# One input queue for the loads and a choice of VectorE or GpSimd for SBUF-only steps, in an attention and feed-forward kernel

## The chip, the cores and the metric

The kernel runs on one core of one Trainium2 chip. The metric is device time in microseconds (us), lower is better. The engines are named as the profile names them: PE is the TensorE matmul, PEld its weight load, DVE is VectorE, ACT is ScalarE, POOL is GpSimd, SP is SyncE, which only issues DMAs here. PSUM is the memory that PE writes; SBUF is the other on-chip memory.

## The reference, cut to what matters

The input `x` has 2048 tokens of width 512. There are 32 heads of width 16, and four segments of 512 tokens. Each segment has causal attention within itself and, from the second on, reads a memory that the earlier segments left. A gated feed-forward layer (GEGLU, inner width 1792) runs beside it, and a gate per token mixes the two.

```python
phi = lambda t: jnp.where(t > 0, t + 1.0, jnp.exp(t))      # the feature map
g = _sigmoid(beta).reshape(1, H, 1, 1)                     # one number per head
for s in range(N):                                         # N = 4 segments
    p = _softmax(qs @ ks^T * scale + mask)                 # written out as einsums in the reference
    a_dot = p @ vs
    a_mem = (phi(qs) @ M) / (phi(qs) @ z + 1e-06)
    outs.append(g * a_mem + (1.0 - g) * a_dot)
    M = M + phi(ks)^T @ vs;  z = z + sum(phi(ks))
a = concat(outs) @ wo
b = (gelu(x @ w_gate) * (x @ w_up)) @ w_down
gt = _sigmoid((x * gate_w).sum(-1))
return gt * a + (1 - gt) * b
```

## The kernel before

The kernel is a list scheduler. It builds a graph of tasks, each with an engine and an estimated time, simulates the engines and the DMA, and emits each engine's instructions in the order that it found. On the chip every engine then runs its list strictly in that order.

```python
def schedule(self):
    ...
    for e in ENGINES:
        for t in ready[e]:                       # a task may be ready on several engines
            st = max(cur[e], ready_at[t.id])
            ...
            k = (st, -t.prio - ..., t.id)        # the earliest possible start wins
    ...
    t.finish = st + t.est[e]
    avail = t.finish
    if t.nbytes:                                 # a DMA: bytes at one rate, in issue order
        dma_free = max(t.finish + 1.5, dma_free) + t.nbytes / DMA_RATE
        avail = dma_free
```

The first is the loads at the start, with `betaT`, the second layout of `beta`, loaded by four DMAs that write 2 elements (4 bytes) at a time:

```python
for a in range(4):
    rank[0] -= 20.0                              # rank: the wished-for order of the loads
    dma(f"x0_{a}", SP, ..., 131072, bias=rank[0])
wdma("wk", ACT, wk[:], r4(A_wk), 524288)         # ACT issues these two, SP the others
wdma("wq", ACT, wq[:], r4(A_wq), 524288)
...
for g in range(4):                               # no rank: they end up last
    bsrc = A_beta.rearrange("(t g j) -> g t j", g=4, j=2)[g]
    dma(f"betaT{g}", SP, lambda g=g: betaT[32 * g:32 * g + 32, :].rearrange("p (t j) -> p t j", j=2),
        lambda bsrc=bsrc: bsrc.partition_broadcast(32), [], [("betaT", g)], 1024, nonc=True)
```

```python
exp_task(0, "gexp", [
    Instr(lambda e: e.activation(gexp[:], betab[:], ACTF.Exp), ...),
    Instr(lambda e: e.activation(gexpT[:], betaT[:], ACTF.Exp), ...)])
task("gmat", DVE, [...])                         # 1 / (1 + exp), two layouts
```

The DVE work that touches only SBUF: the feature map (two one-input steps and a two-input add per half), the masked copies of K (`kpad`), the masked memory (`mzbd`) and the final add of attention and memory:

```python
task(f"{nm}c{s}_{i}", DVE, [
    Instr(lambda e: e.tensor_scalar(dst[:, t0:t1, :], src[:, t0:t1, :], 0.0, None, ALU.max), ...),
    Instr(lambda e: e.tensor_scalar(ex[:], ex[:], 1.0, None, ALU.min), ...),
    Instr(lambda e: e.tensor_tensor(dst[:, t0:t1, :], dst[:, t0:t1, :], ex[:], ALU.add), ...)])
```

POOL, before, does little but the causal masks (an affine-select on each block of exponentials).

The softmax here doesn't subtract the row's maximum and nothing guards it: scores larger than these inputs give would overflow.

Of the kernel before, what the change touches and what calls it, by code (L numbers as in the profile page):

```python
# [12 lines left out]
ALU = mybir.AluOpType  # L13
# [4 lines left out]
DF = 1792  # L18
# [306 lines left out]

def pool_sel_t(n):
    return 0.17 + n * 0.00105
# [7 lines left out]
def _build(es, nc, A_x, A_wq, A_wk, A_wv, A_wo, A_beta, B_w_gate, B_w_up, B_w_down, gate_w, out):  # L335
# [70 lines left out]

    def mm(g, view, lhsT, rhs, reads, first, last, n, fkey=None):
        return Instr(lambda e: e.matmul(view(), lhsT, rhs, start=first, stop=last),  # L408
                     reads=reads, writes=[fkey if fkey is not None else g.key], est=mm_t(n))
# [60 lines left out]
    for a in range(4):  # L470
        rank[0] -= 20.0
        dma(f"x0_{a}", SP, lambda a=a: xin[:, a, :], lambda a=a: A_x[0, a * 128:(a + 1) * 128, :], [],
            [("hT", 1, a)], 131072, bias=rank[0])
    wdma("wk", ACT, wk[:], r4(A_wk), 524288)
    wdma("wq", ACT, wq[:], r4(A_wq), 524288)
    wdma("gatew", ACT, gatew[:], gate_w.rearrange("(kb p) -> p kb", p=P), 1024, nonc=True)
    wdma("wv", SP, wv[:], r4(A_wv), 524288)
    wdma("beta", SP, betab[:], A_beta.partition_broadcast(P), 8192)
    for g in range(4):
        bsrc = A_beta.rearrange("(t g j) -> g t j", g=4, j=2)[g]  # L480
        dma(f"betaT{g}", SP, lambda g=g: betaT[32 * g:32 * g + 32, :].rearrange("p (t j) -> p t j", j=2),
            lambda bsrc=bsrc: bsrc.partition_broadcast(32), [], [("betaT", g)], 1024, nonc=True)
    wdma(("wg", 0), SP, wg[:, :, 0:half], wgr[:, :, 0:half], 917504)
    xdma(1)
    wdma(("wg", 1), SP, wg[:, :, half:DF], wgr[:, :, half:DF], 917504)
# [7 lines left out]
    for i in range(8):  # L493
# [4 lines left out]
    for kb in range(4):  # L498
# [5 lines left out]
                 [("xT", 0, kb)], 512)  # L504

# [24 lines left out]
    def exp_task(phase, name, instrs, **kw):  # L530
# [3 lines left out]
        t = task(name, ACT, instrs, after=after, **kw)  # L534
        exp_tasks[phase].append(t)
# [23 lines left out]
    def phi_task(nm, s, phase, src, skey, dst, dkey, i):  # L559
# [7 lines left out]
        task(f"{nm}c{s}_{i}", DVE, [  # L567
            Instr(lambda e: e.tensor_scalar(dst[:, t0:t1, :], src[:, t0:t1, :], 0.0, None, ALU.max), tk, dk,
                  dve_t(1024, 4)),
            Instr(lambda e: e.tensor_scalar(ex[:], ex[:], 1.0, None, ALU.min), [("pex", i)], [("pex", i)],  # L570
                  dve_t(1024, 4)),
            Instr(lambda e: e.tensor_tensor(dst[:, t0:t1, :], dst[:, t0:t1, :], ex[:], ALU.add),
                  dk + [("pex", i)], dk, dve_t(1024, 2))])

    def prep(s):
# [11 lines left out]
        if s > 0:  # L587
            for j in range(2):
                task(f"kp{s}_{j}", DVE, [
                    Instr(lambda e, j=j: e.tensor_scalar(kpad[j][sl][:], kT[:], maskc[j][:, 0:1], None, ALU.mult),  # L590
                          [("kT", t) for t in range(4)] + [("c", "mask", j)],
                          [("kpad", j, sl, t) for t in range(4)], dve_t(2048, 4, ap=True))])
# [66 lines left out]
    def memory(s):  # L659
        sl = s % 2  # L660
        if s < NSEG - 1:
# [5 lines left out]
            for i in range(2):  # L667
# [10 lines left out]
                else:  # L678
# [3 lines left out]
                task(f"mzbd{s}_{i}", DVE, [  # L682
                    Instr(lambda e, i=i: e.tensor_tensor(
                        MZbd[:, 2 * i:2 * i + 2, :], MZacc[:, 2 * i:2 * i + 2, :],
                        bdmask[:, :].rearrange("p (o c) -> p o c", o=1).to_broadcast([P, 2, 136]), ALU.mult),
                        [("MZacc", i), ("c", "bd")], [("MZbd", 2 * i), ("MZbd", 2 * i + 1)], dve_t(272))])
# [4 lines left out]
    def attention(s):  # L691
        sl = s % 2
        for t in range(4):
# [53 lines left out]
            def norm():  # L747
# [14 lines left out]
                    Instr(lambda e: e.transpose(dst, obf[i2][:]), [("obf", i2)], dk, dve_t(512))]  # L762
                if s > 0:
# [210 lines left out]
```

## Time and profile before

Three runs have a median of 298.05 us (297.53 to 298.47).

| | before |
|---|---|
| median, us | 298.05 |
| span of the profiled run, us | 296.6 |
| PE busy, us (share) | 277.6 (94%) |
| DVE busy, us | 193.1 (65%) |
| ACT busy, us | 215.6 (73%) |
| POOL busy, us | 102.5 (35%) |

From the page of the kernel before, the line of busy times and the clock that was granted to PE, in tenths of full speed, in 40 slices of 7.4 us:

```profile
PE 277.6 (94%) x2185; PEld 115.2 (39%) x2185; DVE 193.1 (65%) x335; ACT 215.6 (73%) x169; POOL 102.5 (35%) x193
...
PEclk9799999999999999996999999999999999999999
```

PE is the bottleneck, at 94%. What can be won is PE's idle time and the two dips of its clock, in the second slice and near 135 us. The view of waits, for PE of the kernel before (columns: who waited, for whom, us in total, how often, the longest):

```profile
PE psXALL L703 <- ACT pt L711: 4.8, 6, 1.3
PE psW L408 <- DVE hT L834: 2.6, 3, 1.6
PE psW L408 <- DVE otok L650: 2.4, 5, 1.7
PE psW L500 <- DMA hT<-in_A_x_dram: 2.4, 2, 1.9
```

Two stretches of PE's timeline show what the change aims at. Columns: start, duration, engine, line, operation, and in brackets the idle time before it and what ended it. The start:

```profile
7.58 0.23 PE L500 MATMUL psW<-ident,hT 128*128 128x128 bf16 x1 [1.86 <-DMA hT<-in_A_x_dram]
8.30 1.53 PE L500 MATMUL psW<-ident,hT 128*128 128x128 bf16 x13 [0.49 <-DMA hT<-in_A_x_dram]
9.62 1.06 PE L408 MATMUL psW<-xT,wk 128*128 128x512 bf16 x2
10.47 1.06 PE L408 MATMUL psW<-xT,wq 128*128 128x512 bf16 x2
```

`x` is the last thing to arrive, and the first K matmuls take 0.43 us each (two of them pass from 9.62 to 10.47) where warm ones take 0.216. The stage near 130 us:

```profile
133.38 0.39 PE L703 MATMUL psXALL<-qT,kpad_1 32*128 32x512 bf16 x4 [1.35 <-ACT pt L711]
135.42 1.20 PE L408 MATMUL psW<-mzbd,phq 128*128 128x128 bf16 x8 [1.65 <-DVE otok L650]
```

Here PE waits for DVE's `otok`, and directly before it DVE's list holds one of the SBUF-only steps that the change offers to POOL (a final add, at 133.61 us, of 1.15 us).

### The profile page before, as it was taken

To read this page: it belongs to the slowest core of one execution; us is meant where nothing else is said; L and a number is where in the kernel's file an instruction comes from. 1 tells how busy PE (TensorE), PEld (TensorE's weight loads), DVE (VectorE), ACT (ScalarE), POOL (GpSimd) and SP (SyncE) were. 2 spreads that over 40 slices of the span, in tenths; PEclk is the share of its full clock that TensorE was granted. 3 is DMA by queue.
4 is the path that set the end of the run, shared out by engine and by line. 5 is a ranking of instruction groups with operands and counts; after the bars stand their busy time and mean duration, and the time that the engine had idled before them with its cause. 6 is when DMAs were issued, how large, how long until landed. Compare 5 with 4: busy or idle time off the path is not lost.

```text
span 296.6 us, 5371 instructions
## 1 busy us (share of the span) xinstructions
PE 277.6 (94%) x2185; PEld 115.2 (39%) x2185; DVE 193.1 (65%) x335; ACT 215.6 (73%) x169; POOL 102.5 (35%) x193
## 2 busy tenths in 40 slices
PE   5999999998899999987998999997998999997995
PEld 1443433334443344342443334433443334333442
DVE  0388899678988655796427783869616773559431
ACT  2387898889999877877579697687768677667202
POOL 7026773341004346733003334563202334433200
PEclk9799999999999999996999999999999999999999
DMA  7999920000024201002002100110003000000002
GB/s 217 246 338 352 114 49 2 0 1 2 18 55 88 56 24 43 7 2 53 2 5 48 38 0 0 38 39 0 2 1 73 2 0 20 35 20 0 2 0 71
DMA packets 29769, 15.30 MB, mean 52 GB/s; under 512 B 21296, under 2 KB 29744, under 8 KB 29744
## 3 DMA queue, kind: packets, MB, share of 16 engines
q1 hardware_dynamic: 28160, 13.91, 18.8%
q10 hardware_dynamic: 1584, 1.05, 1.2%
q8 instruction: 17, 0.28, 0.4%
q14 instruction: 8, 0.07, 0.1%
HBM read 8.14 MB, written 2.10 MB: 35 GB/s over the span
## 4 chain that ended last, share of the span: by engine, by line
PE 74%; ACT 11%; DVE 9%; DMA 2%; issue 2%; SPq 0%; POOL 0%; ACTq 0%; DVEq 0%
PE psW L408 59%; PE psXALL L703 8%; PE psP L736 6%; ACT pt L711 5%; ACT hT L802 3%; DMA hT<-in_A_x_dram 2%; PE psXALL L408 1%; ACT L711 1%; DVE vaug L425 1%; DVE hT L834 1%; DVE kpad_0 L582 1%; DVE kT L425 1%; DVE tb L744 1%; DVE obf L760 1%; DVE kpad_1 L590 1%
## 5 line engine op out<-in xcount | busy, mean ns | idle before, releaser
L711 ACT ACTIVATE pt<-psXALL 128x2048 bf16<-128x2048 f32 x80 | 150.1, 1876 | 45.0 <-PE psXALL L703 33.5
L723 POOL TENSOR_SCALAR_AFFINE_SELECT pt<-pt 128x512 bf16<-128x512 bf16 (+1 forms) x112 | 83.5, 747 | 171.7 <-ACT pt L711 165.0
L408 PE MATMUL psW<-xT,wu 128*128 128x512 bf16 x224 | 53.0, 380 | 4.0 <-DVE hT L834 2.1
L408 PE MATMUL psW<-xT,wg 128*128 128x512 bf16 x224 | 53.0, 389 | 0.0
L408 PE MATMUL psW<-wd,hT 128*128 128x512 bf16 x210 | 50.7, 380 | 0.0
L834 DVE TENSOR_TENSOR hT<-psW,hT 128x512 bf16<-128x512 f32 x56 | 37.7, 686 | 8.6 <-PE psW L408 8.0
L744 DVE STREAM_TRANSPOSE tb<-psP 128x512 f32<-128x512 f32 x32 | 22.8, 713 | 22.8 <-PE psP L736 22.7
L408 PEld LDWEIGHTS psW<-xT,wg 128*128 128x128 bf16 x224 | 21.0, 100 | 27.2 <-issue 4.9
L408 PEld LDWEIGHTS psW<-xT,wu 128*128 128x128 bf16 x224 | 19.8, 98 | 28.9 <-DVE hT L834 3.2
L408 PEld LDWEIGHTS psW<-wd,hT 128*128 128x128 bf16 x210 | 18.9, 97 | 23.7 <-issue 3.6
L736 PE MATMUL psP<-pt,vaug 128*17 128x256 bf16 (+3 forms) x512 | 23.6, 305 | 0.0
L813 ACT ACTIVATE hT<-psW 128x512 bf16<-128x512 f32 x28 | 16.5, 597 | 8.1 <-PE psW L408 8.1
L862 DVE TENSOR_SCALAR ost<-psW,omgt 128x512 bf16<-128x512 f32 x12 | 8.7, 743 | 16.7 <-PE psW L408 16.7
L703 PE MATMUL psXALL<-qT,kpad_1 32*128 32x512 bf16 (+3 forms) x256 | 16.1, 305 | 2.6 <-ACT pt L711 2.4
L703 PE MATMUL psXALL<-qT,kpad_0 32*128 32x512 bf16 (+3 forms) x256 | 15.8, 301 | 2.4 <-ACT pt L711 2.4
L408 PE MATMUL psW<-xT,wk 128*128 128x512 bf16 x64 | 17.0, 395 | 0.1
L408 PE MATMUL psW<-xT,wq 128*128 128x512 bf16 x64 | 16.6, 388 | 0.3 <-DVE qT L425 0.3
L650 DVE TENSOR_TENSOR otok<-psW,ndsc 128x512 bf16<-128x512 f32 x12 | 7.6, 683 | 13.2 <-PE psW L408 13.1
L408 PE MATMUL psW<-wo,oT 128*128 128x512 bf16 x60 | 15.8, 380 | 0.0
L408 PE MATMUL psW<-wv,xT 128*128 128x512 bf16 x64 | 15.5, 380 | 0.0
L736 PEld LDWEIGHTS psP<-pt,vaug 128*17 128x17 bf16 x512 | 10.1, 90 | 13.4 <-issue 6.6
L425 DVE CAST hT<-psW 128x512 bf16<-128x512 f32 x20 | 13.2, 676 | 2.6 <-PE psW L408 2.6
(90 smaller groups left out, 252.6 us busy)
## 6 DMA issues: line engine op xcount, KB each, us to landing
out_dram<-ost SPq DMA_DIRECT2D x16, 128.0 KB, 1.7
wg<-in_B_w_gate_dram SPq DMA_DIRECT2D x2, 896.0 KB, 7.7
wu<-in_B_w_up_dram SPq DMA_DIRECT2D x2, 896.0 KB, 8.2
wd<-in_B_w_down_dram SPq DMA_DIRECT2D x1, 1792.0 KB, 14.9
wk<-in_A_wk_dram ACTq DMA_DIRECT2D x1, 512.0 KB, 4.2
hT<-in_A_x_dram SPq DMA_DIRECT2D x4, 128.0 KB, 5.0
wq<-in_A_wq_dram ACTq DMA_DIRECT2D x1, 512.0 KB, 6.1
wv<-in_A_wv_dram SPq DMA_DIRECT2D x1, 512.0 KB, 8.5
```

Of the source, the lines that this page charges most:

```text
L408: return Instr(lambda e: e.matmul(view(), lhsT, rhs, start=first, stop=last), reads=reads, writes=[fkey if fkey is not None else g.key], e ...
L425: alts[DVE] = [Instr(lambda e: e.tensor_copy(dst(), src()), reads=reads, writes=writes, est=dve_t(n))]
L650: Instr(lambda e, gn=gn, qt=qt: e.tensor_tensor(otok[:, qt, :].rearrange("p (h e) -> p h e", e=16), gn.f32()[:, :].rearrange("p (h e) -> p ...
L703: instrs.append(Instr(lambda e, t=t, g=g, j=j, kb=kb, ncol=ncol, c0=c0: e.matmul(X[g][:, c0:c0 + ncol], kpad[j][sl][32 * g:32 * g + 32, t, ...
L711: prev_exp[0] = exp_task(s, f"exp{s}_{t}{name}", [Instr(lambda e: e.activation(PT[slot][:], XALL[:, :].rearrange("p (g c) -> p g c", g=4), ...
L723: minstrs.append(Instr(lambda e, view=view, pat=pat: e.affine_select(out=view, in_=view, compare_op=ALU.is_ge, fill=0.0, base=0, pattern=p ...
L736: instrs.append(Instr(lambda e, q=q, kb=kb, slot=slot, c0=c0, h=h: e.matmul(Pb[32 * q:32 * q + 17, 128 * kb:512], Vaug[sl][:, kb, h, :], P ...
L744: task(f"pvt{s}_{t}_{j}", DVE, [Instr(lambda e: e.transpose(Tb[i2][:, j, :], Pb[:, :]), [("P",)], [("Tb", i2, j)], dve_t(512))])
L802: t = task(f"gelu{s}_{f0}", ACT, [Instr(lambda e, hv=hv: e.activation(hv, hv, ACTF.Gelu_apprx_tanh), hk, hk, act_t(512 * n, False) + (0.0 ...
L813: lambda e, g=g, ft=ft, s=s: e.activation(hT[s % 2][:, ft, :], g.f32()[:, :], ACTF.Gelu_apprx_tanh),
L834: task(f"Um{s}_{ft}", DVE, [Instr(lambda e, g=g, ft=ft: e.tensor_tensor(hT[sl][:, ft, :], g.f32()[:, :], hT[sl][:, ft, :], ALU.mult), [g.k ...
L862: DVE: [Instr(lambda e, view=view, gt=gt, tile=tile: e.tensor_scalar(ostage[tile][:], view(), omgt[:, gt:gt + 1], None, ALU.mult), rd, [(" ...
```

## The change

It has two intents. The first is to have `x` land sooner: all input loads go on SP's queue in one order, `x` first in two larger loads, and the small loads of the gates follow the weights of Q, K and V. A few more idle matmuls keep PE's clock up until `x` is there. The second is to unload DVE: each SBUF-only step becomes its own task with two alternatives, and the scheduler takes whichever engine can start it first. The diff, cut to its core:

```diff
+def pool_t(n, two=False):
+    return 0.2 + n * (0.0022 if two else 0.0011)

+    def either(name, fn, reads, writes, dve, pool, **kw):
+        return S.add(Task(name, {DVE: [Instr(fn, reads, writes, dve)], POOL: [Instr(fn, reads, writes, pool)]}, **kw))

-    for a in range(4):
+    for a in range(2):
...                                       # x in two loads of 256 KB
-    wdma("wk", ACT, wk[:], r4(A_wk), 524288)
-    wdma("wq", ACT, wq[:], r4(A_wq), 524288)
-    wdma("gatew", ACT, gatew[:], ...)
+    wdma("wk", SP, wk[:], r4(A_wk), 524288)
+    wdma("wq", SP, wq[:], r4(A_wq), 524288)
     wdma("wv", SP, wv[:], r4(A_wv), 524288)
+    wdma("gatew", SP, gatew[:], ...)
     wdma("beta", SP, betab[:], A_beta.partition_broadcast(P), 8192)
     for g in range(4):
+        rank[0] -= 20.0
         dma(f"betaT{g}", SP, ...,
-            ..., [], [("betaT", g)], 1024, nonc=True)
+            ..., [], [("betaT", g)], 1024, nonc=True, bias=rank[0])
     wdma(("wg", 0), SP, wg[:, :, 0:half], wgr[:, :, 0:half], 917504)
+    wdma(("wg", 1), SP, wg[:, :, half:DF], wgr[:, :, half:DF], 917504)
     xdma(1)
-    wdma(("wg", 1), SP, wg[:, :, half:DF], wgr[:, :, half:DF], 917504)

-        task(f"{nm}c{s}_{i}", DVE, [ max, min, add ])             # abridged
+        either(f"{nm}r{s}_{i}", max,  ..., dve_t(1024, 4), pool_t(1024))
+        either(f"{nm}m{s}_{i}", min,  ..., dve_t(1024, 4), pool_t(1024))
+        either(f"{nm}a{s}_{i}", add,  ..., dve_t(1024, 2), pool_t(1024, True))
...                                       # likewise kpad (in halves), mzbd, the final add (nadd)
```

(The diff also adds three warm matmuls before the first K matmul and 1.3 us to the estimate of one exp in each segment after the first.) With these estimates the scheduler moves 28 steps to POOL: 13 one-input steps of 128x1024, and 15 with two inputs (6 feature-map adds, 7 final adds of 128x512, 2 memory masks). And because every estimate enters one simulation, the whole order changes.

More of the change, by code (lines that the diff above doesn't have):

```diff
@@ L469, in _build @@
     xin = hT[1][:, 0:4, :]
-    for a in range(4):
+    for a in range(2):
         rank[0] -= 20.0
-        dma(f"x0_{a}", SP, lambda a=a: xin[:, a, :], lambda a=a: A_x[0, a * 128:(a + 1) * 128, :], [],
-            [("hT", 1, a)], 131072, bias=rank[0])
-    wdma("wk", ACT, wk[:], r4(A_wk), 524288)
-    wdma("wq", ACT, wq[:], r4(A_wq), 524288)
-    wdma("gatew", ACT, gatew[:], gate_w.rearrange("(kb p) -> p kb", p=P), 1024, nonc=True)
+        dma(f"x0_{a}", SP, lambda a=a: xin[:, 2 * a:2 * a + 2, :],
+            lambda a=a: A_x[0, a * 256:(a + 1) * 256, :].rearrange("(t p) d -> p t d", p=P), [],
+            [("hT", 1, 2 * a), ("hT", 1, 2 * a + 1)], 262144, bias=rank[0], issue=0.45)
+    wdma("wk", SP, wk[:], r4(A_wk), 524288)
+    wdma("wq", SP, wq[:], r4(A_wq), 524288)
     wdma("wv", SP, wv[:], r4(A_wv), 524288)
+    wdma("gatew", SP, gatew[:], gate_w.rearrange("(kb p) -> p kb", p=P), 1024, nonc=True)
     wdma("beta", SP, betab[:], A_beta.partition_broadcast(P), 8192)
@@ L480, in _build @@
         bsrc = A_beta.rearrange("(t g j) -> g t j", g=4, j=2)[g]
+        rank[0] -= 20.0
         dma(f"betaT{g}", SP, lambda g=g: betaT[32 * g:32 * g + 32, :].rearrange("p (t j) -> p t j", j=2),
-            lambda bsrc=bsrc: bsrc.partition_broadcast(32), [], [("betaT", g)], 1024, nonc=True)
+            lambda bsrc=bsrc: bsrc.partition_broadcast(32), [], [("betaT", g)], 1024, nonc=True, bias=rank[0])
     wdma(("wg", 0), SP, wg[:, :, 0:half], wgr[:, :, 0:half], 917504)
+    wdma(("wg", 1), SP, wg[:, :, half:DF], wgr[:, :, half:DF], 917504)
     xdma(1)
-    wdma(("wg", 1), SP, wg[:, :, half:DF], wgr[:, :, half:DF], 917504)
     wdma(("wu", 0), SP, wu[:, :, 0:half], wur[:, :, 0:half], 917504)
@@ L492, in _build @@
                              [("P",)], 0.43)], bias=5001.0)
-    for i in range(8):
+    for i in range(9):
         gw = Grp(banks)
@@ L504, in _build @@
                  [("xT", 0, kb)], 512)
+    task("warmE", PE, [Instr(lambda e: e.matmul(Pb[:, :], warm[:, 0:128], warm, start=True, stop=True), [wkey],
+                             [("P",)], 0.3) for _ in range(3)], bias=4.0,
+         after=[t for t in S.tasks if t.name == "x0t3"])
     c = [Instr(lambda e: e.memset(maskc[0][:], 0.0), writes=[("c", "mask", 0)], est=0.1)]
@@ L534, in exp_task @@
         t = task(name, ACT, instrs, after=after, **kw)
+        if phase > 0 and name.endswith("_0A0"):
+            t.est[ACT] += 1.3
         exp_tasks[phase].append(t)
@@ L566, in phi_task @@
                                                tk, [("pex", i)], act_t(1024, False))])
-        task(f"{nm}c{s}_{i}", DVE, [
-            Instr(lambda e: e.tensor_scalar(dst[:, t0:t1, :], src[:, t0:t1, :], 0.0, None, ALU.max), tk, dk,
-                  dve_t(1024, 4)),
-            Instr(lambda e: e.tensor_scalar(ex[:], ex[:], 1.0, None, ALU.min), [("pex", i)], [("pex", i)],
-                  dve_t(1024, 4)),
-            Instr(lambda e: e.tensor_tensor(dst[:, t0:t1, :], dst[:, t0:t1, :], ex[:], ALU.add),
-                  dk + [("pex", i)], dk, dve_t(1024, 2))])
+        either(f"{nm}r{s}_{i}", lambda e: e.tensor_scalar(dst[:, t0:t1, :], src[:, t0:t1, :], 0.0, None, ALU.max),
+               tk, dk, dve_t(1024, 4), pool_t(1024))
+        either(f"{nm}m{s}_{i}", lambda e: e.tensor_scalar(ex[:], ex[:], 1.0, None, ALU.min), [("pex", i)],
+               [("pex", i)], dve_t(1024, 4), pool_t(1024))
+        either(f"{nm}a{s}_{i}", lambda e: e.tensor_tensor(dst[:, t0:t1, :], dst[:, t0:t1, :], ex[:], ALU.add),
+               dk + [("pex", i)], dk, dve_t(1024, 2), pool_t(1024, True))
     def prep(s):
@@ L588, in prep @@
             for j in range(2):
-                task(f"kp{s}_{j}", DVE, [
-                    Instr(lambda e, j=j: e.tensor_scalar(kpad[j][sl][:], kT[:], maskc[j][:, 0:1], None, ALU.mult),
-                          [("kT", t) for t in range(4)] + [("c", "mask", j)],
-                          [("kpad", j, sl, t) for t in range(4)], dve_t(2048, 4, ap=True))])
+                for i in range(2):
+                    tt = (2 * i, 2 * i + 1)
+                    either(f"kp{s}_{j}{i}", lambda e, j=j, i=i: e.tensor_scalar(
+                        kpad[j][sl][:, 2 * i:2 * i + 2, :], kT[:, 2 * i:2 * i + 2, :], maskc[j][:, 0:1], None,
+                        ALU.mult), [("kT", t) for t in tt] + [("c", "mask", j)],
+                        [("kpad", j, sl, t) for t in tt], dve_t(1024, 4, ap=True), pool_t(1024))
         for tile in range(4):
@@ L681, in memory @@
                 task(f"mzacc{s}_{i}", DVE, [first], grp=gm)
-                task(f"mzbd{s}_{i}", DVE, [
-                    Instr(lambda e, i=i: e.tensor_tensor(
-                        MZbd[:, 2 * i:2 * i + 2, :], MZacc[:, 2 * i:2 * i + 2, :],
-                        bdmask[:, :].rearrange("p (o c) -> p o c", o=1).to_broadcast([P, 2, 136]), ALU.mult),
-                        [("MZacc", i), ("c", "bd")], [("MZbd", 2 * i), ("MZbd", 2 * i + 1)], dve_t(272))])
+                either(f"mzbd{s}_{i}", lambda e, i=i: e.tensor_tensor(
+                    MZbd[:, 2 * i:2 * i + 2, :], MZacc[:, 2 * i:2 * i + 2, :],
+                    bdmask[:, :].rearrange("p (o c) -> p o c", o=1).to_broadcast([P, 2, 136]), ALU.mult),
+                    [("MZacc", i), ("c", "bd")], [("MZbd", 2 * i), ("MZbd", 2 * i + 1)], dve_t(272),
+                    pool_t(272, True))
     pt_next = [0]
@@ L762, in norm @@
                     Instr(lambda e: e.transpose(dst, obf[i2][:]), [("obf", i2)], dk, dve_t(512))]
+                task(f"norm{s}_{t}", DVE, ins)
                 if s > 0:
-                    ins.append(Instr(lambda e, t=t: e.tensor_tensor(oT[sl][:, t, :], oT[sl][:, t, :], ott[i2][:],
-                                                                    ALU.add), ok + dk, ok, 0.7))
-                task(f"norm{s}_{t}", DVE, ins)
+                    either(f"nadd{s}_{t}", lambda e, t=t: e.tensor_tensor(oT[sl][:, t, :], oT[sl][:, t, :],
+                                                                         ott[i2][:], ALU.add),
+                           ok + dk, ok, 0.5, pool_t(512, True))
             a0 = fill("A0", [(0, 0, 512, 0)], [0])
```

## The prediction

> What bounds the kernel now. The page gives PE 277.6 us busy of 296.6 (94%); the chain that ended last is 74% PE, 11% ACT, 9% DVE. So only PE's idle 19 us and its cold-clock time can be won. PE's timeline places the idle time:
> - Start: 1.3 us, then about 2.6 us for x (four loads, the last lands at 8.25 us, sharing DMA with wk and wq). Afterwards PE runs cold: matmuls at 0.43 us against 0.216, until 12.1 us.
> - 74 to 81 us: 2.0 us (V eviction behind a gelu on ACT, then DVE's numerators).
> - 130 to 136 us: 3.0 us (exp, then DVE's otok, queued behind a 1.15 us final add); the clock falls to 0.75 and 12 matmuls take 4.4 us instead of 2.7.
> - After gelus: 1.05 (157 us), 0.79 (226 us); 1.6 at 204; 1.6 at 273 (DVE); end about 3 us.
>
> What the change does.
> 1. x goes first, alone, in two loads on one queue, then wk, wq, wv. 512 KB at the 340 GB/s seen later is 1.5 us; x should land near 5 us instead of 8.25. More warm matmuls bridge it. The first K matmul should start at 7 to 7.5 us instead of 9.6, warm. Gain 2 to 3.5 us. Cost: x of segment 1 now queues behind both gate halves and the tiny gate and beta loads; I estimate it at 17 to 21 us, needed at about 20: risk of a stall up to 1.5 us.
> 2. By the instruction orders, about 30 steps move from DVE to POOL: 13 one-input 1024-wide steps, 6 two-input adds, 7 final adds, 2 memory masks. DVE loses about 19 of 193 us (0.42 to 0.7 each). POOL's affine-select of 512 takes 0.65, of 1024 1.1 us, so one-input steps should take about 1.3; for two inputs the Trainium skill, "GPSIMD Engine Reference", section 3.1, states 2.6 cycles an element: an estimate of 2.4 us per 1024. POOL grows from 102 to about 145 us. The skill's "SBUF — State Buffer", "two separate sides", says that GpSimd and a DVE operation with two SBUF inputs or in a two-port mode exclude each other; the trace agrees in kind (an add of mean 0.62 took 1.15 beside a mask). So some DVE steps lengthen and some masks come 1 to 2 us late, mostly absorbed by six buffers.
> 3. The schedule reorders: memory and numerators of segment 1 leave the gelu phase, whose up-projections then run unbroken (gain about 1.7); they land in the stage near 110 us, where ACT's exps are denser than PE's work, so I expect about 2 us idle there instead of the 3 us and the cold clock (gain 1 to 2). Five up-projections, instead of three, cover the table load and first exp after the second gelu (gain 1). DVE waits near 165 and 273 shrink (gain 1 to 1.5).
>
> Sum: gains 7.5 to 10, new losses 1 to 3. Predicted 291.0 us, 8 in 10 between 287.0 and 295.0. Faster by over 2% (under 292.1): 0.60; within 2%: 0.37; slower: 0.03.
>
> What would show it: x landed near 5 us; K matmuls at 0.216 us from the start; PE busy little changed but idle near 12 us; DVE near 175, POOL near 145; no clock dip at 130 to 140; the wait for ACT after the second gelu gone.
>
> What would make it wrong: x of segment 1 late; POOL adds much over 2.4 us or masks delayed so that attention waits for POOL; the numerator stage near 110 us idling PE long enough to drop the clock again; the scheduler's order fitting the chip badly.

## More of the kernel before

`beta` is 32 numbers, and the kernel needs it in two layouts; two small ACT exps and five tiny DVE steps use `beta` and `betaT`.

## The result, and the profile after

The changed kernel is slower: a median of 314.8 us (314.29 to 316.64, 4 runs) against 298.26 (297.53 to 298.51, 4 runs) for the kernel before, with the outputs correct in both. The ratio is 1.057, with a 95% interval of 1.0523 to 1.0617. Ratios are the mean time of one kernel's runs over that of the other's runs of the same rounds, so they are not quite the ratio of the medians that are quoted. Executions over 1.5% slower than the fastest of the same kernel are left out of the means.

| | before | after | predicted |
|---|---|---|---|
| median, us | 298.26 | 314.8 | 291.0 |
| span of the profiled run, us | 296.6 | 312.6 | |
| PE busy, us | 277.6 | 282.5 | little changed |
| span less PE busy, us | 19.0 | 30.1 | about 12 |
| DVE busy, us | 193.1 | 188.7 | about 175 |
| POOL busy, us | 102.5 | 162.7 | about 145 |
| mean granted clock | 0.983 | 0.966 | |

From the page of the changed kernel, the same lines as before:

```profile
PE 282.5 (90%) x2189; PEld 114.9 (37%) x2189; DVE 188.7 (60%) x316; ACT 214.5 (69%) x166; POOL 162.7 (52%) x221
...
PEclk9959999999999999887999999999779999999999
```

PE lost both ways: 11.1 us more idle, and 4.9 us more busy, as its clock dips in three places, near 20, 135 and 225 us (a slice is 7.8 us here). Those are the places of the stories below. PE's waits, after:

```profile
PE psXALL L719 <- DVE gtmp L561: 6.3, 1, 6.3
PE psW L416 <- DVE hT L851: 6.1, 7, 3.3
PE psXALL L719 <- ACT pt L727: 4.5, 8, 1.8
PE psW L416 <- DVE kT L433: 3.5, 2, 3.2
PE psP L752 <- POOL pt L739: 1.5, 2, 0.7
```

Three waits of over 3 us are new: 6.3 (at 18 us), 3.2 (at 141 us) and 3.3 (at 224 us).

**The start.** `x` now lands near 5 us and K's matmuls run warm from 7.46 us, as predicted. Then ACT stops. ACT's timeline after:

```profile
8.54 0.60 ACT L430 ACTIVATE kT<-psW 128x512 bf16<-128x512 f32 x1 [1.84 <-PE psW L416]
10.98 0.23 ACT L554 ACTIVATE gexp<-betab 128x32 f32<-128x32 bf16 x1 [1.84 <-DMA betab<-in_A_beta_dram]
17.25 0.21 ACT L555 ACTIVATE gexpT<-betaT 128x8 f32<-128x8 bf16 x1 [6.05 <-DMA betaT<-in_A_beta_dram]
17.37 0.58 ACT L430 ACTIVATE qT<-psW 128x512 bf16<-128x512 f32 x1
...
18.81 1.88 ACT L727 ACTIVATE pt<-psXALL 128x2048 bf16<-128x2048 f32 x1 [0.38 <-PE psXALL L719]
```

The two gate exps stand in ACT's list between the first K eviction and the evictions of Q and K that attention needs. They wait for `betaT` until 17.25 us, so the copy of Q out of PSUM waits too. PE's wait is put down to DVE's `gtmp`, a gate step that ended at 17.95 us, but the matmul that it ends in reads `qT`, and the eviction of `qT` by ACT ended at the same moment (17.37 + 0.58 = 17.95): the releaser in such a line is inferred, and what the instruction reads decides. DVE's list stops too, for 7.7 us, as its five gate steps wait for `gexpT`. The first attention exp starts at 18.81 us instead of 15.22 before. The chain of waits shows the load behind it, from its issue to its landing (columns: start, duration, what):

```profile
7.56 9.58 DMA betaT<-in_A_beta_dram
...
17.25 0.22 ACT gexpT L555
...
18.09 0.62 PE psXALL L719 x4
```

Four loads of 512 bytes each take until 17.1 us. Busy times by windows of 2 us (columns: busy us of each engine, then the granted clock, the share of the 16 DMA engines that was busy, and GB/s):

```profile
10.00:12.00 2.00, 1.75 (x9) 0.59 (x6) 0.00 (x0) 0.23 (x1) 0.00 (x0) 1.00 0.06 1
12.00:14.00 2.00, 0.00 (x0) 0.00 (x0) 0.00 (x0) 0.00 (x0) 0.00 (x0) 1.00 0.03 0
14.00:16.00 2.00, 0.00 (x0) 0.00 (x0) 0.00 (x0) 0.00 (x0) 0.00 (x0) 0.78 0.54 190
16.00:18.00 2.00, 0.00 (x0) 0.00 (x0) 0.44 (x4) 0.75 (x3) 0.00 (x0) 0.50 0.98 376
```

For 4 us the input queue moves next to nothing, with a DMA share of 0.03 to 0.06, about one engine of the 16; then no engine computes at all; and the clock falls to 0.50 after the idle time. The packets that the trace records, by size and microsecond of the span (a count, not a view of the profile):

```
us   packets started
 9   68 of 1024 B, 171 of 2 B, 44 of 64 B, 80 of 4 B
10   107 of 4 B, 22 of 64 B, 11 of 2 B
11   110 of 4 B
12   57 of 4 B
13   90 of 4 B
14   94 of 4 B, 56 of 1792 B
15   28 of 4 B, 156 of 1792 B
```

`betaT` is 4 loads x 32 partitions x 4 runs of 4 bytes, 512 such packets (some of the 566 of 4 B counted here are not `betaT`'s: up to 18 in a microsecond start before any `betaT` load is issued). They take 7 to 8 ns each, and their times add up to 0.4 to 0.8 us in each microsecond, less than one of the 16 engines can give; in the trace about a third of them (107 of 316 between 10 and 14 us) overlap the next. Small size alone doesn't explain the rate: the 512 packets of 2 B, which are `gatew`, went faster, 330 of them in the microsecond from 8 us. The gate weights (1792 B), which stand behind `betaT` on the same queue, start at 14.2 us, when most of its packets are through.

**POOL.** The groups of moved instructions after, by shape (columns: busy us and mean ns of one, then POOL's idle time before them and what ended it):

```profile
L582 POOL TENSOR_SCALAR phq<-qT 128x1024 bf16<-128x1024 bf16 x4 | 11.5, 2872 | 0.6 <-PE psW L416 0.6
L584 POOL TENSOR_SCALAR pex<-pex 128x1024 bf16<-128x1024 bf16 x4 | 11.2, 2809 | 0.6 <-ACT pex L580 0.6
L586 POOL TENSOR_TENSOR phq<-phq,pex 128x1024 bf16<-128x1024 bf16 x5 | 10.9, 2182 | 0.0
L605 POOL TENSOR_SCALAR kpad_1<-kT,maskc 128x1024 bf16<-128x1024 bf16 x3 | 8.8, 2940 | 3.8 <-ACT kT L430 3.0 <-DVE kT L433 0.9
```

A one-input step takes 2.8 to 2.9 us on POOL. The scheduler was told 0.2 + 1024 x 0.0011 = 1.33, and the prediction said 1.3. A two-input step takes 2.18, where the scheduler was told 2.45 and the prediction 2.4. What the 2.8 does is seen before the wait at 141 us:

```profile
131.75 2.77 POOL L582 TENSOR_SCALAR phq<-qT 128x1024 bf16<-128x1024 bf16 x1
134.48 0.63 POOL L739 TENSOR_SCALAR_AFFINE_SELECT pt<-pt 128x512 bf16<-128x512 bf16 x1
135.09 2.76 POOL L582 TENSOR_SCALAR phq<-qT 128x1024 bf16<-128x1024 bf16 x1
137.82 2.11 POOL L586 TENSOR_TENSOR phq<-phq,pex 128x1024 bf16<-128x1024 bf16 x1
137.88 2.60 DVE L586 TENSOR_TENSOR phq<-phq,pex 128x1024 bf16<-128x1024 bf16 x1 [3.89 <-POOL phq L582]
140.40 0.68 DVE L433 CAST kT<-psW 128x512 bf16<-128x512 f32 x1
141.14 0.82 PE L416 MATMUL psW<-xT,wu 128*128 128x512 bf16 x2 [3.24 <-DVE kT L433]
```

Read from the top: POOL does two slow `max` steps. DVE's next step is the add that needs the second, so DVE, the engine that was to be relieved, stands idle for 3.89 us. It then starts that add beside POOL's own add of the other half, and takes 2.60 us for what takes 0.68 alone. Only then can it evict K, and PE waits 3.24 us for the bank. The wait at 224 us, likewise:

```profile
213.41 2.91 DVE L605 TENSOR_SCALAR kpad_1<-kT,maskc 128x1024 bf16<-128x1024 bf16 x2
213.76 2.28 POOL L586 TENSOR_TENSOR phq<-phq,pex 128x1024 bf16<-128x1024 bf16 x1
...
219.39 2.12 POOL L586 TENSOR_TENSOR phq<-phq,pex 128x1024 bf16<-128x1024 bf16 x1
219.72 1.84 DVE L774 TENSOR_TENSOR sc_0<-recip,gdT 128x32 f32<-128x32 f32 x1
...
224.48 1.89 PE L416 MATMUL psW<-xT,wu 128*128 128x512 bf16 x4 [3.27 <-DVE hT L851]
```

A DVE step of 128x32, which took 0.19 us at 129.48 us, takes 1.84 us and ends with POOL's add. The evictions behind it come late, and PE waits. This is why DVE's busy time fell by only 4.4 us although 28 steps left it: the steps that stayed got longer. (In e2, below, where the 28 steps are back on DVE in the same order, they take about 16 us by their means, and DVE's total is 189.2. So the steps that stayed took about 16 us more here.)

### The profile page after: what moved, and what is told of

The parts are those of the page before. It is cut to its first block, busy times and chain, and to the rows that moved or that the text cites. A ratio compares the mean times of both kernels' runs of the same rounds, so it can differ in the third digit from the quotient of the medians.

```text
span 312.6 us, 5382 instructions
## 1 busy us (share of the span) xinstructions
PE 282.5 (90%) x2189; PEld 114.9 (37%) x2189; DVE 188.7 (60%) x316; ACT 214.5 (69%) x166; POOL 162.7 (52%) x221
## 4 chain that ended last, share of the span: by engine, by line
PE 67%; POOL 11%; DVE 8%; ACT 4%; DMA 4%; issue 3%; SPq 2%; ACTq 0%; DVEq 0%; POOLq 0%
PE psW L416 54%; PE psXALL L719 7%; PE psP L752 5%; POOL pt L739 4%; POOL exsT L634 3%; DMA betaT<-in_A_beta_dram 3%; ACT pt L727 3%; POOL phq L582 3%; SPq L447 1%; PE psXALL L416 1%; DVE hT L851 1%; DVE obf L776 1%; POOL kpad_0 L605 1%; DVE tb L760 1%; DMA oT<-otok 1%
## 5 line engine op out<-in xcount | busy, mean ns | idle before, releaser
L739 POOL TENSOR_SCALAR_AFFINE_SELECT pt<-pt 128x512 bf16<-128x512 bf16 (+1 forms) x112 | 85.2, 763 | 107.7 <-ACT pt L727 99.9
L416 PE MATMUL psW<-xT,wu 128*128 128x512 bf16 x224 | 55.3, 391 | 9.4 <-DVE hT L851 5.9
L719 PE MATMUL psXALL<-qT,kpad_0 32*128 32x512 bf16 (+3 forms) x256 | 16.3, 308 | 7.4 <-DVE gtmp L561 6.3
L719 PE MATMUL psXALL<-qT,kpad_1 32*128 32x512 bf16 (+3 forms) x256 | 16.3, 309 | 3.5 <-ACT pt L727 3.5
L416 PE MATMUL psW<-wv,xT 128*128 128x512 bf16 x64 | 17.3, 410 | 0.7 <-DVE ost L879 0.5
L433 DVE CAST hT<-psW 128x512 bf16<-128x512 f32 x22 | 14.6, 677 | 3.7 <-PE psW L416 3.5
L416 PE MATMUL psW<-xT,wq 128*128 128x512 bf16 x64 | 15.8, 380 | 0.8 <-DMA wq<-in_A_wq_dram 0.5
L781 POOL TENSOR_TENSOR oT<-oT,ott 128x512 bf16<-128x512 bf16 x7 | 8.2, 1174 | 16.0 <-DVE ott L778 15.0
## 6 DMA issues: line engine op xcount, KB each, us to landing
wg<-in_B_w_gate_dram SPq DMA_DIRECT2D x2, 896.0 KB, 12.5
```

The costliest lines, as they stand in the source:

```text
L416: return Instr(lambda e: e.matmul(view(), lhsT, rhs, start=first, stop=last), reads=reads, writes=[fkey if fkey is not None else g.key], e ...
L433: alts[DVE] = [Instr(lambda e: e.tensor_copy(dst(), src()), reads=reads, writes=writes, est=dve_t(n))]
L719: instrs.append(Instr(lambda e, t=t, g=g, j=j, kb=kb, ncol=ncol, c0=c0: e.matmul(X[g][:, c0:c0 + ncol], kpad[j][sl][32 * g:32 * g + 32, t, ...
L739: minstrs.append(Instr(lambda e, view=view, pat=pat: e.affine_select(out=view, in_=view, compare_op=ALU.is_ge, fill=0.0, base=0, pattern=p ...
L781: either(f"nadd{s}_{t}", lambda e, t=t: e.tensor_tensor(oT[sl][:, t, :], oT[sl][:, t, :], ott[i2][:], ALU.add), ok + dk, ok, 0.5, pool_t(5 ...
```

## The experiments

The theory had two independent parts. S: the start loses because the gate exps stand in ACT's list before the evictions and wait for `betaT`. P: the rest loses because steps on POOL are slow and block DVE. The rivals were R, the new order is bad in itself, whatever the engines do; D, the loads alone are at fault (what queues behind the tiny packets); and, within P, whether the one-input steps (longer than thought) or the two-input steps (which exclude DVE) do the harm. Two kinds of edit were used. In the first the changed kernel's schedule is computed as it is, and one thing is then moved in the finished order or between the two engines; the rest of the order stays, and the emitter adds the waits that the new order needs. In the second an estimate or the code is changed and the schedule computed anew, which changes the order too.

All kernels gave correct outputs. The runs were made on four chips, each beside the kernel before, whose median was 297.76 to 298.61 us; a difference of under 1 us between two is not read.

### e1_gexp_later: the gate steps later in the order

```diff
-    for t in S.schedule():
+    order = S.schedule()
+    late = [t for t in order if t.name in ("gexp", "gmat")]
+    order = [t for t in order if t not in late]
+    at = [t.name for t in order].index("gexs0")
+    order[at:at] = late
+    for t in order:
```

The loads stay where the change put them; only the two ACT exps and the five DVE steps are emitted later.

> The schedule of the changed kernel is kept; only the two gate exponentials on ScalarE and the five small gate steps on VectorE, which wait for the late beta load, are moved behind the fourth exp of the first attention stage. Every DMA stays where it is. Theory A (in-order engines ScalarE and VectorE stood 6 us behind the beta load, 17.25 us): the first exp starts at 12 to 13 us instead of 18.8, and the time falls by 4 to 6 us, to about 310. Rival (the loads themselves are late, not the wait on them): the PE waits for DMA instead and the time falls by under 2 us.

Measured: 309.53 us (309.24 to 310.11), ratio 1.0404 (1.0381 to 1.0426). The wait of 6.3 us is gone from PE's waits. So 5.3 of the 16.5 us come from the place of these seven small instructions in the order. A new wait appears, though: 2.8 us for `xT`, the input of segment 1, which stands behind the tiny packets and the gate weights on the queue, and the clock falls to 0.83 over 20 to 30 us. That is rival D, and e6 takes it up.

### e2_all_dve: no step on POOL

```diff
+    for t in order:
+        if len(t.alts) == 2 and DVE in t.alts and POOL in t.alts:
+            t.eng = DVE
```

> The order is kept, but the 29 steps that the scheduler gave to GpSimd run on VectorE at the same place in the order; the beta loads stay. Theory B (GpSimd one-input steps of 2.8 us and the port exclusion delay masks, kT, phq and the up-projection evictions): PE idle of about 10 us at 42 to 49, 131, 141 and 224 us goes, time falls by 8 to 11 us to about 305. Rival (the order of the scheduler is bad whatever the engine; VectorE gets 19 us more work): falls by under 4 us.

Measured: 302.34 us (301.69 to 302.93), ratio 1.0159 (1.0133 to 1.0185). Moving the 28 steps (the expectation miscounted them as 29) back to DVE, in the same order, is worth 12.5 us, a little more than the 8 to 11 expected, and the clock dips near 140 and 220 us are gone. DVE's busy time is 189.2 us, against 188.7 with POOL's help: the 28 steps cost DVE nothing net.

### e3_both: both edits

> Both edits, order otherwise kept. If A and B are all of the loss and add up: 314.8 minus 5 minus 10, about 299 to 301, near the kernel before. If there is a third cause (order, x of segment 1 late): stays above 303.

The edit is that of e1 and of e2 together. Measured: 298.7 us (297.66 to 299.69), ratio 1.0047 (1.0006 to 1.0087). The two parts make 16.1 us together and 17.7 one by one, so they are nearly additive, and between them they account for nearly the whole loss. Rival R is refuted as the cause of the slowdown: this is the changed kernel's own order, but for the seven small steps, and it is within 1% of the kernel before. That the order is a good one is not shown by this; b1 below finds one that is about 7 us faster.

### a1_beta_late: the tiny loads at the end of the queue, scheduled anew

```diff
     for g in range(4):
-        rank[0] -= 20.0
         dma(f"betaT{g}", SP, ...,
-            ..., [], [("betaT", g)], 1024, nonc=True, bias=rank[0])
+            ..., [], [("betaT", g)], 1024, nonc=True)
```

> The four tiny beta loads go to the end of the input queue as before (one line undone), and the scheduler makes its order anew; GpSimd steps stay. Theory A with the tiny loads also holding up the queue: the gate weights land near 15 us instead of 20, the first exp starts near 12 us, time 308 to 310. Rival: same as in the moved-exponential run would mean that the queue hold-up itself costs nothing.

Measured: 306.67 us (304.68 to 308.99), ratio 1.0308 (1.025 to 1.0366). The start was repaired, but this is a partial miss: the same wait came back in another place. The line of PE's timeline in a1_beta_late:

```profile
36.84 1.46 PE L416 MATMUL psW<-xT,wg 128*128 128x512 bf16 x3 [4.96 <-ACT exs L622]
```

Its chain of waits goes from there to `gexpT` on ACT and to a `betaT` load that took 8.76 us after its issue at 27.65. The scheduler still believes that 1024 bytes need next to nothing, so it again put the gate exps before the loads had landed. The fault is the estimate, not only the place in the queue.

### e4_one_dve and e5_two_dve: which kind of step

The order stays. In e4 the 13 one-input steps go back to DVE and the 15 two-input steps stay on POOL; e5 is the reverse.

```diff
+    ONE = ("pqr", "pqm", "pkr", "pkm", "kp")
+    TWO = ("pqa", "pka", "mzbd", "nadd")
+    for t in order:
+        if len(t.alts) == 2 and DVE in t.alts and POOL in t.alts:
+            if t.name.startswith(ONE):        # e5: TWO
+                t.eng = DVE
```

> Order of the changed kernel kept, beta loads kept; the 13 one-input steps (2.8 us each on GpSimd) go back to VectorE, the 15 two-input ones (2.1, 1.2 and 0.7 us) stay on GpSimd. If the cost is the long one-input steps holding up GpSimd's own queue (masks, phq, kT): most of the 12.5 us comes back, about 304 to 306. If it is the exclusion of VectorE's two-input steps while GpSimd does a two-input step: little comes back, 311 to 314.

> The reverse: the 15 two-input steps go back to VectorE, the 13 one-input steps stay on GpSimd. If GpSimd's own queue is the cost: 309 to 313, PE idle near 131 and 141 us stays. If exclusion by two-input steps is the cost: 303 to 306, and the PE idle of 3.3 us near 224 us goes.

Measured: e4 305.91 us (305.68 to 306.4), ratio 1.0277 (1.0256 to 1.0297); e5 309.76 us (309.12 to 310.19), ratio 1.04 (1.0379 to 1.0421). Against 314.8 the one-input steps are worth 8.9 us and the two-input steps 5.0, which add up to 13.9 where both together gave 12.5. Each of the two stalls follows one kind. In e4 PE's waits for `kT` fall from 3.5 us to 0.2, and the wait before the matmul of the second stall stays:

```profile
217.02 1.04 PE L416 MATMUL psW<-xT,wu 128*128 128x512 bf16 x4 [3.27 <-DVE hT L851]
```

In e5 it is the first that stays, and the second becomes shorter (2.0 us is the longest of its kind):

```profile
139.23 0.61 PE L416 MATMUL psW<-xT,wu 128*128 128x512 bf16 x2 [2.74 <-DVE kT L433]
```

So both kinds harm, the one-input steps more, and in different places.

### e6_beta_mid: the tiny loads behind the input of segment 1

The order and engines are those of e3 (no POOL steps). In addition the four `betaT` loads move behind `x` of segment 1, just before the up weights, and what needs them moves back accordingly.

```diff
+    move(("betaT0", "betaT1", "betaT2", "betaT3"), "w_('wu', 0)")
+    move(("gexp", "gmat", "GdT0"), "gexs1")
```

> The run with both edits (298.7) had 2.5 us of PE waiting for x of segment 1 at 20 us and a cold clock after it, and the input queue moved nothing but 4-byte packets from 10 to 14.5 us. Here the four beta loads also go behind x of segment 1, ahead of the up weights, and what needs them behind that; all steps on VectorE. If the tiny loads hold up the whole queue: gate weights land some 4.5 us sooner, the PE wait at 20 us goes, no cold clock at 20 to 30 us, time 294 to 296. If x of segment 1 is late because it queues behind both gate halves: wait stays, time 298 to 299.

Measured: 295.78 us (295.54 to 296.33), ratio 0.9935 (0.9918 to 0.9952), 2.9 us under e3. The stretch at which e3 waited for the input, first in e3_both, then in e6_beta_mid:

```profile
22.88 3.75 PE L416 MATMUL psW<-xT,wq 128*128 128x512 bf16 x8 [2.49 <-DMA xT<-in_A_x_dram]
```

```profile
23.32 1.90 PE L416 MATMUL psW<-xT,wq 128*128 128x512 bf16 x8
```

Eight matmuls take 3.75 us in e3, after an idle time and at a granted clock of 0.57 (mean from 23 to 27 us), and 1.90 in e6, where the clock in that stretch is 1.00. The hold-up by the tiny packets is still there (the DMA share over 20 to 25 us is 0.20), but nothing that PE needs stands behind it. So D is a real but smaller part: about 3 us.

### m1_micro: single steps, alone and side by side

The kernel before, followed by a tail that runs single steps of 128x1024 (bf16) on POOL and DVE, alone, then together. Its time (334.58 us) says nothing; only the tail's lines are read. In the pairs DVE starts 0.2 to 0.4 us after POOL. Each entry is a single sample, and the profiler's spans on POOL are rough.

```diff
+        PH = [(p_ts, None), (p_tt, None), (p_ts5, None), (p_tt5, None), (p_tsm, None), (p_cp, None), (p_sel, None),
+              (None, d_ts), (None, d_tt), (None, d_ps),
+              (p_ts, d_ts), (p_ts, d_tt), (p_ts, d_ps), (p_tt, d_ts), (p_tt, d_tt), (p_tt, d_ps),
+              (p_sel, d_ts), (p_sel, d_tt), (p_sel, d_ps)]
```

> Not for its time: the kernel before, with single steps of GpSimd and VectorE after its end, each alone and then together (VectorE starting about 0.3 us later). Expected alone on 128x1024 bf16: GpSimd one input 2.8, two inputs 2.1, select 1.1; VectorE one input 0.4, two inputs 0.7, from PSUM 0.7. Together: VectorE's two-input step grows to the end of GpSimd's two-input step (about 2.3 us) and of the select; VectorE's step from PSUM is not touched. Open: whether VectorE's one-input step, and its two-input step beside a GpSimd one-input step, are touched[...].

Some lines of the tail's timeline in m1_micro: a one-input POOL step, a two-input one and a select alone; then DVE's two-input step alone and beside POOL's two-input step:

```profile
295.76 2.77 POOL L913 TENSOR_SCALAR pt<-pt 128x1024 bf16<-128x1024 bf16 x1 [17.14 <-DMA out_dram<-ost]
298.68 2.11 POOL L914 TENSOR_TENSOR pt<-pt 128x1024 bf16<-128x1024 bf16 x1
...
308.07 1.05 POOL L919 TENSOR_SCALAR_AFFINE_SELECT pt<-pt 128x1024 bf16<-128x1024 bf16 x1
...
310.35 0.68 DVE L922 TENSOR_TENSOR hT<-hT 128x1024 bf16<-128x1024 bf16 x1
...
323.48 2.11 POOL L914 TENSOR_TENSOR pt<-pt 128x1024 bf16<-128x1024 bf16 x1 [0.36 <-DVE hT L921]
...
323.84 2.30 DVE L922 TENSOR_TENSOR hT<-hT 128x1024 bf16<-128x1024 bf16 x1
```

All of them, in us:

| POOL step | alone | DVE one-input beside it | DVE two-input (SBUF) beside it | DVE with one PSUM input beside it |
|---|---|---|---|---|
| none | | 0.42 | 0.68 | 0.68 |
| one-input max | 2.77 | 0.96 | 1.36 | 0.68 |
| two-input add | 2.11 | 2.17 | 2.30 | 0.68 |
| select | 1.05 | 1.08 | 1.22 | 0.68 |

At 512 elements the one-input step took 1.49 us and the two-input step 1.15, so the slopes are (2.77 - 1.49) / 512 = 2.5 ns and (2.11 - 1.15) / 512 = 1.9 ns per element of a partition. The multiplication by the mask column took 2.85, and a plain copy 1.04. So on POOL a step with one tensor and a scalar costs more than one with two tensors, and of those measured only copy and select are cheap. Beside a two-input add or a select, a DVE step on SBUF ends only after POOL's does. Beside the one-input step it takes 0.5 to 0.7 us more than alone and ends well before POOL does. A DVE step with a PSUM operand is not touched at all. That answers the question left open: DVE's one-input step on SBUF is touched too.

This splits the harm as the stalls do: the one-input steps hurt mainly by their length (the scheduler's 1.33 against 2.8, so what needs them is ready 1.5 us later than planned), the two-input steps by holding DVE up.

### b1_all_dve, b2_true, b4_cheap: mended estimates, scheduled anew

In all three the `betaT` loads stand behind `x` of segment 1 and have a truer cost in the scheduler's DMA model, 700000 bytes each, an estimate that makes the four 8.5 us long at the model's rate.

```diff
     wdma("beta", SP, betab[:], A_beta.partition_broadcast(P), 8192)
+    wdma(("wg", 0), ...); wdma(("wg", 1), ...); xdma(1)      # moved up from below
     for g in range(4):
         rank[0] -= 20.0
-        dma(f"betaT{g}", SP, ..., 1024, nonc=True, bias=rank[0])
+        dma(f"betaT{g}", SP, ..., 700000, nonc=True, bias=rank[0])
```

b1 has only the DVE alternative. b2 keeps both, with the measured POOL costs, `0.2 + n * (0.0019 if two else 0.0025)`. b4 has those costs too but lets only the final adds and memory masks choose (six final adds went to POOL).

> Candidate version: all of the change's start (x first, one queue, warm matmuls, estimate of the table load), the beta loads behind x of segment 1 with a truer cost in the scheduler's estimate, no GpSimd alternative, and the scheduler orders anew. Expected 292 to 295, below both kernels and a little below the frozen order (295.8), because the order is made for the engines that run it. If the order of the scheduler does not matter: 295 to 296.

> As the candidate, but the GpSimd alternatives stay and their estimate is set to what was measured (0.2 + 2.5 ns an element for one input, 1.9 for two). If the cause was only the wrong estimate: as good as the candidate or better, 290 to 294. If holding up masks and VectorE's exclusion cost by themselves: worse than the candidate, 296 to 302.

> As the candidate, but the final add (1.17 us) and the memory mask (0.7 us) may go to GpSimd, with the measured estimate. Six final adds go there. VectorE loses about 4 us of work and some of it waits for the exclusion: within 1 us of the candidate.

Measured:

| | median, us (range) | ratio (95%) | POOL busy, us | DVE busy, us |
|---|---|---|---|---|
| b1_all_dve | 288.98 (288.54 to 290.58) | 0.9703 (0.9669 to 0.9736) | 102.6 | 191.0 |
| b2_true | 300.19 (299.0 to 301.52) | 1.007 (1.0028 to 1.0113) | 146.6 | 196.3 |
| b4_cheap | 290.57 (290.06 to 290.82) | 0.9744 (0.9724 to 0.9765) | 110.3 | 187.4 |

b1 beats both kernels: 9.4 us under the kernel before, and 3 us below the range that was expected. It is also 6.8 us under e6 (295.78; other chip, but the ratios' intervals, 0.9669 to 0.9736 and 0.9918 to 0.9952, lie far apart), which has the same loads and no POOL step but the order that was made for the wrong estimates. So that order, too, costs something against one made for the engines that run it. From b1's page, the busy times and the clock, which no longer dips anywhere:

```profile
PE 270.0 (93%) x2151; PEld 114.6 (40%) x2189; DVE 191.0 (66%) x342; ACT 215.3 (75%) x168; POOL 102.6 (36%) x193
...
PEclk9999999999999999999999999999999999999999
```

(38 of PE's matmul records are missing from this trace, so its busy time isn't to be compared with the others; the profiled run was also the slowest of b1's four, 290.58.) b2 is the clear answer to "were only POOL's estimates wrong?": with right costs per step the free choice still loses 11.2 us against b1. The scheduler moved 19 steps, and DVE got busier by 5.3 us instead of less busy. That fits the blocking that m1 shows, of which the scheduler's simulation has no notion; no run puts the blocking into the simulation. b4 shows no gain from the steps that suit POOL best either: its median is 1.6 us above b1's (within 1 was expected), and the intervals of the ratios overlap.

### e7_beta_mid_pool: the tiny loads moved, POOL as in the change

The edit is that of e6 without the last loop, so POOL keeps its 28 steps.

> The changed kernel's order and its GpSimd steps, with only the beta loads and what needs them moved behind x of segment 1. If start and GpSimd add up: 314.8 minus 5.3 minus about 3, near 306.5. If the faster start only runs into the GpSimd queue sooner: 308 to 310.

Measured: the four runs are 309.64, 306.49, 308.48 and 303.69 us, two of them slow by their own spread, and the ratio of the fast ones is 1.0233 (1.0172 to 1.0295). Against e6 (ratio 0.9935) this puts the POOL steps at about 9 us, 7 to 11 by the ends of the two intervals, a little under what e2 gave, but the scatter is too large for more. It is inconclusive on whether the parts add up.

### d1_old_start and d2_beta_front: what in b1 is the start, what the loads' place

d1 is b1 with the input loads of the kernel before (four loads of `x`, two issuing engines, eight warm matmuls, `betaT` without a rank). d2 is b1 with the `betaT` loads back at the place that the change gave them, but with their truer cost in the estimate.

```diff
# d2, against the changed kernel (and only the DVE alternative)
-            ..., [], [("betaT", g)], 1024, nonc=True, bias=rank[0])
+            ..., [], [("betaT", g)], 700000, nonc=True, bias=rank[0])
```

> The candidate (288.98) with the input loads, warm matmuls and two queues of the kernel before; everything else of the candidate stays (split tasks on VectorE, the 1.3 us for the table load, new order). If the one-queue start is worth the 3 us that its first matmuls gained: 292 to 293. If the candidate's gain is all from the start: 297 to 298; if all from the order: 289 to 290.

> The candidate with the beta loads back where the change put them, ahead of the gate weights, but with their true cost in the scheduler's estimate, so that the gate exponentials come after the third exp and do not wait. If only the wait of ScalarE was the harm: 289 to 290. If the 4.5 us hold-up of the queue also harms: x of segment 1 is late, PE waits about 2.5 us at 20 us and runs cold after it, 292 to 293.

Measured: d1 293.86 us (292.56 to 294.8), ratio 0.9844 (0.9808 to 0.9881); d2 291.23 us (289.38 to 292.75), ratio 0.9738 (0.9691 to 0.9786). So the change's new start, with the better place and estimate of `betaT` that b1 adds to it, is worth about 4.9 us of b1 (293.86 - 288.98; other chip, but the intervals of the ratios lie apart). One queue, larger loads and more warm matmuls are not told apart. The rest, the split tasks, the estimate of the table load and the new order, is worth about 4.7 us (298.61, the median of before in that call, less 293.86). For d2 the interval overlaps b1's, so it is inconclusive on whether the place of the tiny loads still matters once the scheduler knows what they cost. Its timeline shows how it copes: it put gate matmuls at 21.9 us, ahead of those that need segment 1's `x`, and no wait for a load follows there.

## Why the prediction was wrong, point by point

The prediction was 291.0 us, 287.0 to 295.0; measured were 314.8. The faster start came as said. It was buried under two losses: a stop of ACT of 5.3 us, which was not foreseen, and the steps on POOL, 12.5 us, where 1 to 3 us had been allowed for all losses together. The gain from reordering, the larger part of the sum, didn't come in this order.

1. **Step 1, the start: the mechanism was right, and a step was left out.** "x should land near 5 us", "the first K matmul should start at 7 to 7.5 us ... warm": 7.46, warm. "Gain 2 to 3.5 us" is even low for what the new start brings in b1's order, where nothing blocks it (about 4.9 us, d1 against b1). What was missed is the order on ACT and DVE. The prediction mentions "tiny gate and beta loads" only as something that `x` of segment 1 queues behind. In the instruction order of the changed kernel, which was at hand, the two gate exps stand directly before the first Q eviction, and in the old one behind seven attention exps. The prediction never asked when their input would land. It landed at 17.1 us, 9.6 us after its last issue, and PE stood for 6.3 us. e1 shows this with the order alone: 5.3 us.

2. **Step 1's risk, `x` of segment 1 "17 to 21 us, needed at about 20: risk of a stall up to 1.5 us": right in kind, too small.** In the changed kernel it was hidden behind the longer stall. With that removed (e1, e3) it is a wait of 2.5 to 2.8 us plus cold matmuls, and e6 measures 2.9 us for it. The prediction counted the tiny loads as bytes, next to none; the runs show about 4.5 us during which the queue moves next to nothing else.

3. **Step 2, "one-input steps should take about 1.3": this term failed.** It was taken from the select, which the profile of before shows at 0.65 and 1.1 us. The select is no guide: measured were 2.77 alone and 2.8 to 2.9 in the kernel, twice the estimate of the prediction and of the change's own cost function. The two-input estimate, 2.4 us from the Trainium skill's "GPSIMD Engine Reference", section 3.1 (about 2.6 cycles per element), agrees well enough: 2.11 alone, 2.18 in the kernel. POOL's total went to 162.7 us, not 145; the 13 one-input steps at 1.5 us above their estimate make about 20 us, more than the whole difference.

4. **Step 2's cost, "some DVE steps lengthen and some masks come 1 to 2 us late, mostly absorbed by six buffers", in the sum "new losses 1 to 3": this is the largest error.** Measured is 12.5 us (e2). The prediction knew that the engines exclude each other and even quoted an add that took 1.15 us beside a mask, and yet it subtracted 19 us from DVE as if nothing came back. DVE's busy time fell by 4.4. And the harm is not in the buffers of the masks, where it was looked for. It is in DVE's list: DVE waits for POOL's result (3.89 us), is blocked (2.60 for 0.68), and PSUM evictions that PE needs come behind. The waits of PE for POOL itself are 1.5 us in all.

5. **Step 3, the reordering, gains of 4.7 to 6.2 us by its own terms: not borne out in this order.** Single places are as predicted: after the second gelu the wait is gone, and the up-projections of the first gelu phase run unbroken. But in the stretch near 120 us e6, without POOL's steps, has PE idle for 3.1 us (0.46 + 0.37 + 1.34 + 0.91 in 118 to 124), where "about 2" was expected, and its clock is 0.5 from 123.4 to 126.8 us, as the prediction had feared. With both obstacles and the late load out of the way, the changed kernel's order is 2.1 us under the kernel before (e6: 295.78 against 297.86 in the same call), less than the start alone is worth in b1. So no gain from this order is shown. The gain of about 4.7 us in d1 is that of another order, scheduled anew for DVE alone. The clock dip at 130 to 140 was there in the changed kernel, with another at 223; of the kernels without POOL's steps e2 and b1 have none in that stretch, e3 and e6 have one earlier (at 126 and 123), and d1 and d2 still have it.

6. **What the text had named as what would make it wrong** was half of it: `x` of segment 1 late (it was, hidden), "POOL adds much over 2.4 us" (the adds were not, the one-input steps were), and attention waiting for POOL (only 1.5 us). That ACT's list would stop for a load of 2 KB in all was not named.

The probabilities said 0.03 for slower. POOL's cost for a one-input step of this size stood in no profile that was at hand, and the whole new order rests on it; that alone should have made the chance of slower larger. The cost of the scattered loads could have been suspected: the list of DMA issues of the kernel before gives `betaT` a median of 7.8 us from issue to landing, for 512 bytes.

What stays open: why the 4-byte packets of `betaT` keep less than one DMA engine busy while those of other loads go faster; what exactly costs a DVE step its 0.5 to 0.7 us beside POOL's one-input step; whether the two causes are strictly additive, for which e7 scattered too much; and what the changed kernel's order by itself costs or gains against that of the kernel before, which no run measured with the old start.

## What to carry to other kernels

Where each engine runs a fixed list, look for every small step that depends on a load and ask what stands behind it in the list: here four element-wise scattered loads, 2 KB in all, held up PE for 6 us. Before handing DVE's work to POOL, measure that very instruction on POOL, alone and beside DVE; in no run here did offloading pay, not even for the six final adds of b4, and a scheduler that knew the durations but not the blocking still chose wrongly (b2). When a change with several parts comes out slow, undo the parts within the same order first; here that found the two causes and a version 0.7% better than the old kernel (e6) inside one that was 5.7% worse. Then schedule anew with what was learnt, which gave 3% (b1).

## What the Trainium skill lacked or had wrong

The pages meant are those of the Trainium skill.

- "GPSIMD Engine Reference", section 4.1 (Engine selection), says that elementwise work with one input is roughly line-rate on GpSimd and only two-input work about twice as slow as on VectorE. Here that holds for copy (1.04 us at 128x1024 bf16) and select (1.05), but not for a tensor with a scalar: 2.77 us for max and 2.85 for a multiplication by a per-partition column, against 0.42 on VectorE and against 2.11 for the two-input add on GpSimd itself. And that add is three times as slow as on VectorE (0.68), not twice.
- "SBUF — State Buffer", section "SBUF: two separate sides", says that of a GpSimd step and a VectorE step in a two-port mode or with two SBUF inputs, whichever starts first has the shared ports for its whole instruction and the other fully blocks. That agrees for a two-input GpSimd step (VectorE 2.17 and 2.30 us instead of 0.42 and 0.68) and for the select (1.08 and 1.22), and a VectorE step with a PSUM operand is free (0.68 beside all of them). It does not agree for GpSimd's one-input step: VectorE ended after 0.96 and 1.36 us while GpSimd ran on to 2.77 (single samples).
- "DMA: Bandwidth & Descriptors", section "Specifications", gives 512 bytes as the smallest transfer at line-rate, and section "Issuing engines are not separate DMA queues" says that issuing from several engines saves only issue time. No page says how far a load of very small runs holds up the loads behind it: here 512 packets of 4 bytes took about 4.5 us, with a DMA share of 0.03 to 0.06 from 10 to 14 us, and the gate weights behind them on the queue waited.
